# Attention plus MLP on one core: the final store as its own last piece, short dummy matmuls around the first transposes, the bias transpose later, and a new hand-written order

## The chip, the cores and the metric

The kernel runs on one core of a Trainium2 chip. The core has TensorE (PE, matrix multiplication; its weight loads are shown as PEld), VectorE (DVE), ScalarE (ACT), GpSimd (POOL) and SyncE (SP). Each works through its own queue in order and waits at semaphores for the others. DMAs are issued from the queues of SP, ACT and POOL. The metric is device microseconds of one execution. Before the change it is 217.93 us, the median of three runs (217.93 to 218.11).

## The reference, cut to what matters

One layer-normalised input feeds a windowed attention and an MLP; both results and the input are added. There are 2048 rows of 640 numbers, 32 heads of 20, and each row attends to 8 rows at distances 0, 2, ... 14 behind it.

```python
S, D, F, H, W, dil = 2048, 640, 1536, 32, 8, 2
xn = (x - mean(x)) / sqrt(var(x) + 1e-5)
q, k, v = split_heads(xn @ wqkv)                 # [H, S, 20] each
logits[h, s, w] = (q[h, s] . k[h, s - 2*w]) * 20**-0.5   # -1e9 where s < 2*w
attn = softmax(logits, axis=w)
o[h, s] = sum_w attn[h, s, w] * v[h, s - 2*w]
out = x + concat_heads(o) @ wo + (gelu(xn @ w1 + b1) @ w2 + b2)
```

All inputs and the output are bf16.

## The kernel before

The 2048 rows are cut into four chunks (0 to 3) of 512, and a chunk into four blocks of 128 rows. Everything on PE, DVE, ACT and SP is issued in an order that stands in the source as a list of piece names, `ORDER`; each name stands for one call of a small function, and each engine gets its instructions in the list's order. The framework adds the semaphores and the waiting for buffers. POOL's queue is not in that list's hands: its adding stores go out as their data become ready.

The names, with n the chunk and b the block in it:

- `st`, `su`, `sq`, `rs`, `rc`: statistics of the layer norm. For chunks 0 and 1 the sums are on DVE (`st`, `bn_stats`, L203), for block 1 of chunk 0 and chunks 2 and 3 on ACT. `rs` is the square root on ACT, `rc` the reciprocal on DVE.
- `xn`: the normalised block; on DVE for chunk 0 (L259), on ACT for the others (L257).
- `tp`, `tc`: for chunk 0 the transposes of xn on PE (L274) and their copies out of PSUM (L279; block 0's are in two parts, a and b, of which a is copied by DVE). In the other chunks `tc` is a transposing DMA issued on SP (L286).
- `ga`, `gb2` to `gb4`, `gd`, `ge`: q projections of blocks 0 and 1 of chunk 0, on PE, 50 matmuls of 128 columns (L331). `gc` copies them out on ACT.
- `hj` w p g and `hc` w p g: the other projections of chunk 0, by w (0 q, 1 k, 2 v), pair of blocks p and group of columns g, on PE with 256 columns (L362), and their copies on ACT (L372). Groups 0 and 1 have ten matmuls, group 2 has five.
- `pj` n w t and `pc` n w t: the projections of chunks 1 to 3, five matmuls of 512 columns each (L318), and their copies on ACT (L377).
- `qk` n b h: products of q with shifted k on DVE, half h of the window (L402). `pa` adds pairs of them (L420). `lg` sums them over the heads on PE into one PSUM tile of the tag L (L429), 24 matmuls, or 40 in chunk 1.
- `m`, `mx`, `ex`, `ss`, `ri`, `at`: the softmax, on DVE except `ex` on ACT. `xd` and `xs` spread attn over partitions by DMA, blocks 0 and 1 from SP, blocks 2 and 3 from ACT (L499).
- `av` n b h: attn times shifted v on DVE (L514); `ad` and `ot` add the products up (L523, L528) to oT.
- `f1` n_t and `ge` n_t: first layer of the MLP, five matmuls of 512 columns (L535), and GELU on ACT (L551).
- `o` n b c: output of a block, in five parts c: second layer of the MLP (0 to 3, three pairs of matmuls each) and the attention's projection (4, five pairs), with 512 columns into `lo` (L571) and 128 into `hi` (L573). For the last block of all the `hi` matmuls are one piece, `ohi`.
- `oc` n b and `od` n b: copy of a finished block to `osb` on ACT (L578, L579) and its adding store to DRAM on POOL (L584). There are two `osb` buffers.
- `oclo` and `ochi`: the last block is finished on DVE, where x is added (L592, L601), and stored plainly, the wide part from SP (L593), the narrow part from ACT (L604).
- `tb` and `b1`: the bias b1 is transposed on PE (L411) and copied by DVE to b1T (L414), which GELU reads.

ACT switches between tables for square root, exponential and GELU; each switch is a table load (L167) of 1.28 us. PSUM has four buffers of the tag acc (projections, first layer, transposes), one each for `lo` and `hi`, and one of the tag L, which the logits, `tb` and the dummy matmuls share.

Ahead of the list stand ten dummy matmuls of 512 columns on a constant of ones (L701), issued before any input has landed. The inputs are loaded from SP in this order: block 0 of x, wq, wk, blocks 2 and 3, wv, blocks 4 to 7, w1; block 1 and b1 from ACT.

## Time and profile before

| | |
|---|---|
| median of three runs | 217.93 us |
| profiled execution, whole | 219.77 us |
| its span, first to last instruction | 217.4 us |
| mean granted clock of PE | 0.994 |
| PE busy | 206.9 us (95%) |
| DVE busy | 179.2 us (82%) |
| ACT busy | 125.4 us (58%) |
| first matmul on a weight (L331) starts | 6.72 us |
| first qk on DVE (L402) starts | 19.34 us |
| ot3, the last large DVE piece, ends | 198.5 us |
| last matmul starts its group | 210.14 us |
| last store issued | 212.46 us |

Times inside the span count from its first instruction. A profile's row of the timeline gives start, length, engine, line, operation, what is written and read, shape, and in brackets how long the engine had been idle and what ended that. Matmuls are pipelined, so the time that one takes on PE is the distance to the start of the next, and the length shown is longer; holes are found from starts. The profiled execution is longer than the timed ones, so differences are worked out in the span and then set against the median.

### The profile page before, as it was taken

Reading aid. Unit: us, or ns where it says so; the run is one execution under the profiler, and the core shown is the slowest. Engines: PE = TensorE matmul, PEld = TensorE weight load, DVE = VectorE, ACT = ScalarE, POOL = GpSimd, SP = SyncE. Lnnn points to the kernel's source line nnn. Section 1 sums busy time; section 2 is a strip of 40 time slices with the busy share of each in tenths; the row PEclk is TensorE's granted clock in tenths of the full one; section 3 lists DMA queues with packets and bytes.
Section 4 is the critical chain, followed back from the end, with each engine's and each line's share of the span. In section 5 each row is a group of like instructions: output and inputs, shape, how many; then the busy total and the mean of one; then the engine's idle time right before and its main releaser. Section 6 shows DMA issues by size and latency. Waiting matters only on the chain.

```text
span 217.4 us, 3276 instructions
## 1 busy us (share of the span) xinstructions
PE 206.9 (95%) x1327; PEld 115.0 (53%) x1327; DVE 179.2 (82%) x166; ACT 125.4 (58%) x239; POOL 19.7 (9%) x37
## 2 busy tenths in 40 slices
PE   8999989999999998999999999999999999999970
PEld 2899635444645554555555544454555455555540
DVE  3578896599799999998999979996999999994010
ACT  5468595999989747689854558631844520111210
POOL 2000000000000500111010400000110101111301
PEclk9999999999999999999999999999999999999997
DMA  6991249418275996015521491702039202222232
GB/s 217 390 398 56 59 108 386 175 18 233 44 142 166 205 186 182 4 29 90 92 30 71 150 175 29 191 5 30 0 39 207 28 13 33 30 30 33 31 59 31
DMA packets 24069, 23.89 MB, mean 110 GB/s; under 512 B 9080, under 2 KB 21880, under 8 KB 24056
## 3 DMA queue, kind: packets, MB, share of 16 engines
q1 hardware_dynamic: 17008, 14.68, 23.3%
q0 software_dynamic: 4144, 4.92, 17.0%
q10 hardware_dynamic: 2904, 4.10, 5.9%
q8 instruction: 10, 0.16, 0.3%
q14 instruction: 3, 0.02, 0.0%
HBM read 10.00 MB, written 7.54 MB: 81 GB/s over the span
## 4 chain that ended last, share of the span: by engine, by line
PE 64%; DVE 13%; issue 11%; ACT 3%; DMA 3%; POOL 2%; ACTq 1%; POOLq 0%; SPq 0%
PE hps L535 19%; PE lo L571 17%; PE pps L318 15%; DVE half L514 5%; PE hi L573 4%; PE gps L362 3%; PE L L429 3%; DVE half L402 3%; DMA wq_sb<-in_A_wqkv_dram 3%; POOL out_dram L584 2%; PE gps L331 2%; DVE half L523 1%; DVE L L451 1%; DVE m L445 1%; ACTq L499 1%
## 5 line engine op out<-in xcount | busy, mean ns | idle before, releaser
L535 PE MATMUL hps<-xnT,w_sb 128*128 128x512 bf16 x240 | 55.4, 379 | 1.3 <-ACT hT L551 0.9
L402 DVE TENSOR_TENSOR half<-qT,kT 128x2560 bf16<-128x2560 bf16 x32 | 45.8, 1484 | 0.7 <-ACT kT L372 0.7
L571 PE MATMUL lo<-w_sb,hT 128*128 128x512 bf16 x144 | 41.0, 379 | 0.0
L535 PEld LDWEIGHTS <-w_sb 128*128 128x128 bf16 x240 | 22.9, 98 | 28.6 <-issue 2.5
L578 ACT CAST osb<-lo 128x512 bf16<-128x512 f32 x15 | 8.8, 585 | 42.7 <-issue 24.6
L573 PE MATMUL hi<-w_sb,hT 128*128 128x128 bf16 x144 | 31.5, 219 | 0.0
L551 ACT ACTIVATE hT<-hps,b1T 128x512 bf16<-128x512 f32 x36 | 23.5, 685 | 11.5 <-PE hps L535 11.5
L514 DVE TENSOR_TENSOR half<-vT,ax 128x2560 bf16<-128x2560 bf16 x16 | 23.1, 1478 | 1.2 <-PE L L429 1.2
L571 PEld LDWEIGHTS <-hT 128*128 128x128 bf16 x144 | 14.1, 98 | 17.2 <-issue 0.4
L571 PE MATMUL lo<-wo,oT 128*128 128x512 bf16 x80 | 23.1, 379 | 0.0
L584 POOL DMA_DIRECT2D out_dram<-osb x15 | 13.0, 864 | 110.0 <-ACT osb L579 94.1
L514 DVE TENSOR_TENSOR half<-vT,x_sb 128x2560 bf16<-128x2560 bf16 x16 | 22.6, 1483 | 0.0
L523 DVE TENSOR_TENSOR half<-half,half 128x5120 bf16<-128x5120 bf16 x8 | 22.3, 2813 | 0.1
L318 PE MATMUL pps<-xnT,wq_sb 128*128 128x512 bf16 x75 | 18.3, 379 | 1.0 <-ACT kT L377 1.0
L318 PE MATMUL pps<-xnT,wk_sb 128*128 128x512 bf16 x75 | 18.5, 379 | 0.0
L318 PE MATMUL pps<-xnT,wv_sb 128*128 128x512 bf16 x75 | 18.0, 379 | 0.0
L167 ACT ACT_TABLE_LOAD x13 | 16.7, 1283 | 1.0 <-PEq L719 0.7
L573 PE MATMUL hi<-wo,oT 128*128 128x128 bf16 x80 | 16.9, 219 | 0.0
L573 PEld LDWEIGHTS <-hT 128*128 128x128 bf16 x144 | 14.1, 98 | 1.7
L420 DVE TENSOR_TENSOR half<-half 128x2048 bf16<-128x2048 bf16 x12 | 14.1, 1216 | 0.0
L318 PEld LDWEIGHTS <-wq_sb 128*128 128x128 bf16 x75 | 8.7, 117 | 8.7 <-issue 1.6
L377 ACT CAST kT<-pps 128x512 bf16<-128x512 f32 x15 | 8.4, 590 | 7.7 <-PE pps L318 4.8
(86 smaller groups left out, 265.4 us busy)
## 6 DMA issues: line engine op xcount, KB each, us to landing
w_sb<-in_B_w_dram SPq DMA_DIRECT2D x4, 960.0 KB, 11.3
out_dram<-osb POOLq DMA_DIRECT2D x15, 160.0 KB, 3.4
out_dram<-b2bc POOLq DMA_DIRECT2D x3, 640.0 KB, 7.1
x_sb<-in_A_x_dram SPq DMA_DIRECT2D x1, 1280.0 KB, 7.8
out_dram<-x_sb ACTq DMA_DIRECT2D x1, 1120.0 KB, 4.8
ax<-attn SPq DMA_DIRECT2D x4, 256.0 KB, 4.3
ax<-attn ACTq DMA_DIRECT2D x4, 256.0 KB, 5.2
x_sb<-attn SPq DMA_DIRECT2D x4, 256.0 KB, 4.5
```

Source lines behind the costliest of these rows:

```text
L167: nc.scalar.activation(warm[:], nc.const_aps.tensor(0.0, [P, 1], F32), func)
L318: nc.tensor.matmul(ps[:], lhsT=wqkv_p[which][:, ti, to, :], rhs=xnT[:, ti, :], start=(ti == 0), stop=(ti == KT - 1),)
L402: nc.vector.tensor_tensor(out=half[h][:, :, :, cs], in0=qkv_tile(n, 0)[:, :, cs].unsqueeze(1).to_broadcast([P, W // 2, KT, P]), in1=window ...
L420: nc.vector.tensor_tensor(out=even, in0=even, in1=odd, op=ALU.add)
L514: nc.vector.tensor_tensor(out=half[h][:, :, :, cs], in0=window(qkv_tile(n, 2), h, cs), in1=ax_view(n)[:, j, ws, :].unsqueeze(2).to_broadca ...
L523: nc.vector.tensor_tensor(out=a, in0=a, in1=b, op=ALU.add)
L535: nc.tensor.matmul(ps[:], lhsT=w1_sb[:, ti, ft * P : (ft + 1) * P], rhs=tiles["xnT", n][:, ti, :], start=(ti == 0), stop=(ti == KT - 1),)
L551: nc.scalar.activation(hT, tiles["hps", n, ft][:], ACT.Gelu_apprx_tanh, bias=b1T[:, ft : ft + 1], scale=1.0)
L571: nc.tensor.matmul(lo[:], lhsT=lhs, rhs=rhs[:, 0:CH], start=first, stop=last)
L573: nc.tensor.matmul(hi[:, 0 : D - CH], lhsT=lhs, rhs=rhs[:, CH:D], start=first, stop=last)
L578: nc.scalar.copy(osb[:, 0:CH], tiles["lo", n, bl][:])
L584: nc.gpsimd.dma_start(rows, tiles["osb", n, bl][:], accum_op=ALU.add)
```

## The change

Five edits, and a new list.

1. The narrow store of the last block leaves `ochi` and becomes a piece of its own, `ochd`, which stands behind `ochi` and behind `oc30` in the new list.
2. The dummy matmuls become a function, `do_warm(n, cols)`. The ten of 512 columns stay, and three of 128 columns follow them ahead of the list.
3. Two new pieces issue more of them: `wa`, one of 128 columns between the transposes `tp00a` and `tp00b`, and `wb`, two of 128 columns behind `tp00b`.
4. `tb` and `b1` move from the middle of the first transposes to behind `ge`.
5. The rest of the list is in another order. The first pieces, to `ge`, keep theirs; behind them nearly all is moved.

```diff
@@ ORDER, its first lines
-pad01 pad02 st00a st00 sum1 rs00 mean1 neg1 rc00 sq1 xn00a xn00b tp00a tp00b tc00a rs01 tb ga tc00b rc01 xn01 gb2 b1
-tp01 gb3 tc01a tc01b gb4 gd gc0 ge st03a st03 rs03 gc1 hj100 st02a rc03 ho hc100 hj101 st02 rs02 hj201 xn03 tp03 rc02
-xn02 st11a st12a st11 st10a gc4 st13a tp02 hc101 tc03 tc02 hc201 hj102 hj200 hc200 hj011 hc102 st10 hc011 st13 st12
-rs1 rc1 qk000 qk001 xn12 tc12 hj112 hc112 xn11 qk011 hj010 hc010 tc11 hj111 hj110 hj202 hc202 hc111 qk010 pa010 hj012
-hc012 hc110 qk021 qk030 qk031 xn10 qk020 pa011 hj211 hc211 tc10 hj212 f10_11 f10_2 xn13 tc13 hc212 ge0_2 f10_9 ge0_9
-f10_0 ge0_0 f10_6 pj114 ldx ld2 pj100 ge0_6 pc100 pj110 pc110 pj102 pad11 pa000 pj112 pa001 lg0 mask m0 ge0_11 pc114
+pad01 pad02 st00a st00 sum1 rs00 mean1 neg1 rc00 sq1 xn00a xn00b tp00a wa tp00b wb tc00a rs01 ga tc00b rc01 xn01 gb2
+tp01 gb3 tc01a tc01b gb4 gd gc0 ge tb b1 st02a hj100 st03a hc100 st02 hj101 rs02 hj200 st03 rs03 gc1 hc101 hc200 rc02
+xn02 ho tp02 gc4 hj202 rc03 tc02 xn03 tp03 st12a st10a st11a tc03 st10 st13a st11 hc202 hj201 hc201 hj102 hc102 hj112
+hj012 hc112 st12 st13 rs1 rc1 qk001 hj212 hc212 xn12 tc12 qk000 qk011 xn11 tc11 hj110 hj111 hc110 hj011 qk010 hc111
+hc012 hc011 hj010 hc010 qk021 f10_3 f10_6 xn10 tc10 xn13 qk020 qk030 f10_0 ge0_0 f10_9 ge0_9 qk031 f10_2 ge0_2 f10_11
+ge0_11 tc13 ldx pj102 ge0_6 pj104 ge0_3 pc102 pj112 pj103 pad11 pa000 pc104 pa011 pa001 pj101 pa010 lg0 pc112 mask m0
...
@@ ORDER, around the second softmax
-f10_8 av030 ge0_8 xn20 f11_5 ge1_5 o001 o002 o003 tc21 ex1 pj122 av021 xp0 xb0 ss1 pj120 xp1 pc122 tc20 pj211 pc211
-xb1 av031 pc120 su32 ri1 ad00 pj204 pc204 at1 xd1 ad01 ad02 ot0 pj203 pad12 av111 pc203 av101 su30 pj222 pc222 pj224
-pc224 pj221 pc221 xs1 av121 pj212 pc212 pj220 pc220 pj223 pj202 pc202 pc223 pj213 pc213 pad22 su33 pj201 f11_1 pc201
+ge0_10 ge0_7 f11_8 ge1_8 tc22 o001 tc20 ex1 f11_5 ss1 av010 ri1 pj120 pc120 ge1_5 o002 o003 av011 at1 xp1 xb1 pj211
+pc211 pj202 ad00 pc202 f11_10 ad01 ad02 pj212 pad12 pj214 su31 pc214 ge1_10 ot0 pad21 pj201 xd1 pc201 pj210 pj223
+pc223 pj222 pc210 pc222 pj221 pc221 av101 xs1 pj213 av121 pc212 pc213 pad31 pj220 pj200 pc220 su32 su30 su33 ng3 av100
...
@@ ORDER, its end
-o323 ot3 o324 oc32 od32 o314 o300 o334 o301 o302 o303 o304 ohi oc31 od31 oclo ochi oc30 od30
+ad31 ad32 ot3 o324 oc32 o314 od22 od32 oc31 od31 o300 o301 o302 o303 o304 oc30 o332 o333 o334 oclo ohi ochi ochd od30
@@ new function
+    ones = nc.const_aps.tensor(1.0, [P, CH], BF16)
+    idle = psL.tile([P, W, P], F32, tag="L", name="idle")
+
+    def do_warm(n, cols):
+        for _ in range(n):
+            nc.tensor.matmul(
+                idle[:].rearrange("p w c -> p (w c)")[:, 0:cols],
+                lhsT=ones[:, 0:P],
+                rhs=ones[:, 0:cols],
+                start=True,
+                stop=True,
+            )
@@ do_ochi and do_ochd
-        nc.scalar.dma_start(out_sd[LASTB * P :, CH:D], osb[:, CH:D])
+
+    def do_ochd():
+        nc.scalar.dma_start(out_sd[LASTB * P :, CH:D], tiles["osb", last][:, CH:D])
@@ pieces
+    piece("wa", do_warm, 1, P)
+    piece("wb", do_warm, 2, P)
@@ ahead of the list
-        ones = nc.const_aps.tensor(1.0, [P, CH], BF16)
-        idle = psL.tile([P, W, P], F32, tag="L", name="idle")
-        for _ in range(WARM):
-            nc.tensor.matmul(idle[:, 0:BPC, :], lhsT=ones[:, 0:P], rhs=ones, start=True, stop=True)
+        do_warm(WARM, CH)
+        do_warm(3, P)
```

More of the change, by code (lines that the diff above doesn't have):

```diff
@@ L44 @@
-f10_0 ge0_0 f10_6 pj114 ldx ld2 pj100 ge0_6 pc100 pj110 pc110 pj102 pad11 pa000 pj112 pa001 lg0 mask m0 ge0_11 pc114
-mx0 pc112 pj111 pc102 su22 su20 ex0 ss0 pj103 pj113 pc103 pc111 pc113 pj104 pc104 pj101 pc101 ri0 at0 f10_1 qk110
-qk130 f11_9 qk120 su23 f10_10 qk101 ge1_9 su21 f11_10 ge0_10 ge0_1 ng2 f11_3 ge1_3 sq21 f10_4 ge0_4 sq23 f11_0 ge1_0
-pj124 pc124 qk121 sq22 f11_7 ge1_7 f10_7 xd0 qk100 qk131 sq20 pj121 ge0_7 rs2 hj210 hc210 qk111 xs0 lg1 ldo rc2 pc121
-xn23 av001 tc23 m1 pj123 pc123 av000 xn22 av010 f10_5 av020 av011 mx1 f11_4 o000 ge0_5 ge1_10 xn21 f10_3 ge0_3 tc22
@@ L49 @@
-f10_8 av030 ge0_8 xn20 f11_5 ge1_5 o001 o002 o003 tc21 ex1 pj122 av021 xp0 xb0 ss1 pj120 xp1 pc122 tc20 pj211 pc211
-xb1 av031 pc120 su32 ri1 ad00 pj204 pc204 at1 xd1 ad01 ad02 ot0 pj203 pad12 av111 pc203 av101 su30 pj222 pc222 pj224
-pc224 pj221 pc221 xs1 av121 pj212 pc212 pj220 pc220 pj223 pj202 pc202 pc223 pj213 pc213 pad22 su33 pj201 f11_1 pc201
-su31 av110 pj210 o004 oc00 od00 pj214 av100 pad21 pc214 pc210 ng3 sq31 av130 o020 o021 av131 av120 o022 o023 sq30 sq32
-o024 oc02 sq33 rs3 rc3 pj200 pc200 xn31 tc31 o030 o031 o032 o033 o034 xn30 tc30 oc03 ad10 od03 f11_6 o010 o011 o012
@@ L54 @@
-ge1_4 xn32 pad31 ad11 tc32 ad12 o013 qk211 xn33 f12_0 o014 f12_4 ge1_1 ge1_6 oc01 od01 ot1 qk221 ge2_0 qk230 qk231
-qk220 qk210 ge2_4 qk201 pa211 pa210 f11_2 ge1_2 tc33 pj320 pj304 pc304 qk200 pa201 pj301 pc301 pj324 pj310 pc324 pa200
-pj303 pc303 pj323 pc323 pad32 pc320 pj312 pj302 xp2 pc302 pj314 pc314 pc312 xl pj313 pj300 pc313 pj311 f13_6 lg2 pc311
-m2 pc310 ge3_6 o130 pc300 qk310 mx2 f11_8 ge1_8 f12_10 o131 o132 qk321 ex2 ss2 ri2 at2 qk301 qk330 qk320 qk331 qk300
-f13_11 pa311 f13_5 ge3_5 f13_10 ge3_10 ge2_10 qk311 ge3_11 f13_4 f13_0 xs2 f13_3 ge3_3 pa300 ge3_4 ge3_0 f11_11 ge1_11
@@ L59 @@
-f12_8 f12_9 pa301 ge2_8 f13_8 ge3_8 pj322 o133 o134 oc13 od13 pc322 f13_1 ge3_1 pa310 o110 o111 o112 lg3 m3 xd2 av210
-xb2 mx3 f12_3 ge2_3 av211 ex3 ss3 f12_7 f13_2 o113 o114 oc11 od11 od02 f13_7 ge3_7 av200 ri3 o100 av230 o101 o102 o103
-xb3 ge3_2 o104 oc10 at3 xs3 f12_6 av231 o120 f12_2 ge2_2 av201 av221 ge2_9 ge2_7 o121 o122 av220 o123 od10 f12_5 ge2_5
-f12_11 o124 oc12 od12 ad20 ad21 ad22 ot2 pj321 pc321 av331 xd3 av300 av301 av321 f12_1 ge2_1 av311 ge2_6 f13_9 o210
-ge3_9 o211 ge2_11 o212 o213 o310 o214 oc21 od21 o330 o331 o200 o201 o202 o203 o204 oc20 od20 o311 o312 o220 o221 o222
@@ L64 @@
-av330 av310 o223 o224 o313 av320 ad30 oc22 od22 ad31 ad32 o230 o231 o232 o233 o234 oc23 od23 o332 o333 o320 o321 o322
-o323 ot3 o324 oc32 od32 o314 o300 o334 o301 o302 o303 o304 ohi oc31 od31 oclo ochi oc30 od30
+pad01 pad02 st00a st00 sum1 rs00 mean1 neg1 rc00 sq1 xn00a xn00b tp00a wa tp00b wb tc00a rs01 ga tc00b rc01 xn01 gb2
+tp01 gb3 tc01a tc01b gb4 gd gc0 ge tb b1 st02a hj100 st03a hc100 st02 hj101 rs02 hj200 st03 rs03 gc1 hc101 hc200 rc02
+xn02 ho tp02 gc4 hj202 rc03 tc02 xn03 tp03 st12a st10a st11a tc03 st10 st13a st11 hc202 hj201 hc201 hj102 hc102 hj112
@@ new lines @@
+hj012 hc112 st12 st13 rs1 rc1 qk001 hj212 hc212 xn12 tc12 qk000 qk011 xn11 tc11 hj110 hj111 hc110 hj011 qk010 hc111
+hc012 hc011 hj010 hc010 qk021 f10_3 f10_6 xn10 tc10 xn13 qk020 qk030 f10_0 ge0_0 f10_9 ge0_9 qk031 f10_2 ge0_2 f10_11
+ge0_11 tc13 ldx pj102 ge0_6 pj104 ge0_3 pc102 pj112 pj103 pad11 pa000 pc104 pa011 pa001 pj101 pa010 lg0 pc112 mask m0
+pc103 pc101 mx0 ld2 pj100 su20 su21 pc100 ex0 ss0 pj111 pj113 pc113 pj114 pc114 pc111 ri0 pj110 pc110 qk101 su23 at0
+qk131 xd0 f11_0 ge1_0 su22 f10_1 f10_5 ge0_5 qk100 qk111 pj122 pc122 ng2 xs0 pj121 f10_8 ge0_8 sq20 f11_3 ge1_3 sq21
@@ new lines @@
+hj211 hc211 qk121 hj210 hc210 pj123 sq22 ge0_1 qk130 qk120 qk110 sq23 ldo pj124 rs2 o000 rc2 pc121 lg1 av031 av021
+av000 xp0 m1 xb0 av001 mx1 f10_4 av020 av030 f10_7 xn21 tc21 pc123 xn23 pc124 ge0_4 xn22 f11_9 tc23 ge1_9 xn20 f10_10
+ge0_10 ge0_7 f11_8 ge1_8 tc22 o001 tc20 ex1 f11_5 ss1 av010 ri1 pj120 pc120 ge1_5 o002 o003 av011 at1 xp1 xb1 pj211
+pc211 pj202 ad00 pc202 f11_10 ad01 ad02 pj212 pad12 pj214 su31 pc214 ge1_10 ot0 pad21 pj201 xd1 pc201 pj210 pj223
+pc223 pj222 pc210 pc222 pj221 pc221 av101 xs1 pj213 av121 pc212 pc213 pad31 pj220 pj200 pc220 su32 su30 su33 ng3 av100
@@ new lines @@
+f11_2 pj204 pc204 av111 av120 pj203 o004 av131 oc00 od00 pad22 pj224 sq33 pc224 sq30 av130 o020 o021 o022 o023 sq32
+o024 f11_11 oc02 o030 o031 o032 o033 sq31 rs3 pc200 av110 od02 rc3 xn32 xn33 tc32 ad11 f11_6 pc203 o034 oc03 od03
+f12_1 o010 o011 o012 o013 ge1_11 f11_4 tc33 xn30 xn31 tc30 tc31 ge2_1 ge1_6 ad10 ad12 o014 qk211 ge1_4 f12_5 ge2_5 ot1
+qk201 qk230 f11_7 pj303 ge1_2 pc303 qk220 pj313 ge1_7 qk200 qk221 pc313 pa210 pj302 pc302 pj300 pc300 qk231 qk210
+pa211 pa200 pj310 pj311 pc311 pj314 oc01 pad32 od01 pc310 pc314 f13_6 pj324 pj320 pc320 pj312 pa201 f11_1 ge3_6 pj304
@@ new lines @@
+ge1_1 xl lg2 pc324 m2 mx2 pc304 pj301 pc301 pc312 qk331 qk320 o130 o131 ex2 ss2 qk321 ri2 at2 xd2 qk311 qk330 o132
+f12_10 f12_6 ge2_6 qk300 f13_11 pa311 qk301 ge3_11 f13_7 ge3_7 f12_4 qk310 pa301 o133 pa310 o134 xp2 ge2_4 oc13 od13
+f13_3 xs2 ge3_3 f13_10 ge3_10 f12_0 f13_1 ge3_1 xb2 f13_5 o120 pj323 o121 o122 o123 o124 oc12 pa300 lg3 pc323 ge3_5 m3
+av201 mx3 av220 ge2_0 ex3 ss3 o110 av210 ri3 av211 f12_7 o111 f13_9 ge3_9 o112 o113 o114 oc11 xb3 f13_0 ge3_0 f13_2
+od11 ge3_2 ge2_7 pj322 pc322 o100 o101 f12_2 ge2_2 od12 f12_11 ge2_11 at3 xd3 av230 f13_8 ge3_8 av221 f12_3 ge2_10
@@ L66 @@
+ge2_3 o102 o103 xs3 av200 f13_4 pj321 pc321 o104 oc10 av231 ad21 ad20 f12_8 ad22 ot2 o210 ge2_8 f12_9 av311 o310 o211
+o212 od10 ge2_9 ge3_4 o213 o214 oc21 od21 av330 o311 o200 av320 o201 o202 o203 av331 av321 av300 o204 oc20 od20 o312
+av301 o230 o231 o232 o233 av310 o234 o313 oc23 od23 o220 o221 o222 o223 o224 oc22 o330 o331 o320 o321 ad30 o322 o323
+ad31 ad32 ot3 o324 oc32 o314 od22 od32 oc31 od31 o300 o301 o302 o303 o304 oc30 o332 o333 o334 oclo ohi ochi ochd od30
 """.split()
@@ L610, in piece @@
         pieces[name] = lambda: fn(*args)
-    for name in "tb b1 mean1 ho ldx ld2 ldo xl oclo ohi ochi mask".split():
+    for name in "tb b1 mean1 ho ldx ld2 ldo xl oclo ohi ochi ochd mask".split():
         piece(name, locals()[f"do_{name}"])
```

## The prediction

> **What bounds the kernel now.** I read the page first (shares, chain), then the tail, the head and the holes of TensorE in order of time.

> ```profile
> PE 206.9 (95%) x1327; PEld 115.0 (53%) x1327; DVE 179.2 (82%) x166; ACT 125.4 (58%) x239; POOL 19.7 (9%) x37
> PE 64%; DVE 13%; issue 11%; ACT 3%; DMA 3%; POOL 2%; ACTq 1%; POOLq 0%; SPq 0%
> out_dram<-osb POOLq DMA_DIRECT2D x15, 160.0 KB, 3.4
> out_dram<-osb SPq DMA_DIRECT2D x1, 128.0 KB, 1.7
> out_dram<-osb ACTq DMA_DIRECT2D x1, 32.0 KB, 1.5
> ```

> TensorE (PE) carries the chain. A 512-column matmul starts every 0.216 us, so its work is fixed; what an order can change is the time before the first one, the holes, and the time after the last. The three store rows price the end: an adding store from POOL lands 3.4 us after issue, a plain one after 1.5 to 1.7. The timeline of the tail (start, length, engine):

> ```profile
> 210.14 0.44 PE L573 MATMUL hi<-wo,oT 128*128 128x128 bf16 x5
> 210.62 0.29 DVE L601 TENSOR_TENSOR osb<-hi,x_sb 128x128 bf16<-128x128 f32 x1 [2.81 <-PE hi L573]
> 210.94 0.35 ACTq L604 DMA_DIRECT2D out_dram<-osb  x1
> 211.41 0.58 ACT L578 CAST osb<-lo 128x512 bf16<-128x512 f32 x1 [6.70 <-DVE osb L601]
> 212.46 0.86 POOL L584 DMA_DIRECT2D out_dram<-osb  x1 [6.59 <-ACT osb L579]
> ```

> PE ends at 210.6 (call it E). The copy oc30 had its sums from o304 by then, but stands behind the store of L604 on ACT and starts at 211.41; its adding store goes out at 212.46 and lands near 215.9. The span ends at 217.4, 1.5 later, which is the closing work. So E to landing is 5.3.

> Head, and the holes of PE:

> ```profile
> 9.00:10.00 1.00, 1.00 (x12) 1.00 (x10) 0.70 (x2) 0.48 (x1) 0.00 (x0) 1.00 1.06 396
> 10.00:11.00 1.00, 1.00 (x21) 1.00 (x19) 0.96 (x4) 0.83 (x2) 0.00 (x0) 1.00 1.07 397
> 9.59 0.89 DVE L203 BATCH_NORM_STATS2 stats<-x_sb 128x6 f32<-128x320 bf16 x2 [0.21 <-DMA x_sb<-in_A_x_dram]
> 11.35 2.35 PE L362 MATMUL gps<-xnT,wk_sb 128*128 128x256 bf16 x20
> 19.34 4.29 DVE L402 TENSOR_TENSOR half<-qT,kT 128x2560 bf16<-128x2560 bf16 x3
> 23.66 0.58 ACT L372 CAST kT<-gps 128x512 bf16<-128x512 f32 x1 [0.69 <-DVE half L402]
> 24.84 1.24 PE L535 MATMUL hps<-xnT,w_sb 128*128 128x512 bf16 x5
> 26.44 3.61 PE L535 MATMUL hps<-xnT,w_sb 128*128 128x512 bf16 x15 [0.36 <-ACT kT L372]
> 30.91 1.24 PE L535 MATMUL hps<-xnT,w_sb 128*128 128x512 bf16 x5 [0.85 <-ACT hT L551]
> 79.50 2.32 PE L318 MATMUL pps<-xnT,wv_sb 128*128 128x512 bf16 x10
> 82.79 1.24 PE L318 MATMUL pps<-xnT,wq_sb 128*128 128x512 bf16 x5 [0.96 <-ACT kT L377]
> ```

> The first two rows are stretches of one microsecond (PE busy and count lead): 12 matmuls of 128 columns to 10.0, 21 after it. Their spacing falls from 107 to 56 ns at 10.0, so PE ran at half speed until then, though the clock column shows 1.00. Holes by spacing: 24.84 + 5 x 0.216 = 25.92, next start 26.44: 0.52. 26.44 + 15 x 0.216 = 29.68, next 30.91: 1.23. 79.50 + 10 x 0.216 = 81.66, next 82.79: 1.13. With 0.2 near 24.7 and 0.2 near 43 that is all of size; elsewhere PE has no hole to win.

> **The change, part by part.** Sums are made on the profiled execution: span 217.4 in 219.77, so 2.35 around it. The timed median, 217.93, is 1.84 below that; I take differences from the span and put them on the median.

> *Last store.* New end: o304, oc30, o332 to o334, ohi, then ochd, last on ACT. oc30 now runs under the 11 lo matmuls and 17 hi matmuls that follow o304: 11 x 0.216 + 17 x 0.056 = 3.33. Its store goes out 1.05 after o304 (211.41 to 212.46 now), at E - 2.3, and lands at E + 1.1. The lo part: o334 ends at E - 0.95, 0.69 on DVE (L592), 1.7 to land: E + 1.5. The hi part: 0.32 to its issue (210.62 to 210.94), 1.5 to land: E + 1.8, the last. So 5.3 becomes 1.8: -3.5; I take **-3.4**. Were the last store to need 3.4 like the adding ones, it would be -1.6. Behind ochd on ACT and SP stands only the closing. The two osb buffers don't bind: oclo needs od31's, which is issued near E - 6.9 and lands at E - 3.5, and oclo starts at E - 0.9.

> *Short matmuls.* Three at the start, at 0.107 (0.32 in all), fill the 0.26 that PE waited for xn at 5.46; the one and the two around the transposes lie before wq, which lands near 6.7 (PE idled 0.35 for it). On the path: 0 to 0.1; if wq came earlier, 0.3. Their gain is unknown. From 6.72 to 10.0 PE issued 31 matmuls at 107 ns; at 56 they would take 1.58 less. So the price lies between 0 and -1.58 (a later opening is excluded: PE does no less before 10.0). I take 0: dense matmuls from 0.78 to 5.05, 4.3 us, did not open the clock before, and this adds 0.64 to them, with transposes in between; what opened it was 3.3 us of dense real work.

> [...]

> *Bias transpose behind the first projections.* This is the costly one. tb on PE now follows ge, and b1 on VectorE (DVE) stands ahead of st02a, st03a and every other statistic. DVE took the rows of x at 9.59 when they landed. Now it waits for ge (11.35), tb 0.19, b1 0.16: it starts near 11.75. From 9.59 to the first qk it needed 9.75, with waits of 1.07 (rstd of block 2) and 0.92 in it; the first goes and about half of the second, since the order of the statistics is better. First qk: 11.75 + 9.75 - 1.07 - 0.45 = 20.0 against 19.34, 0.65 late. PE loses 0.1 for tb.

> *New order at 22 to 32.* Three qk end 4.29 after the first, at 24.3, and hc110, which overwrites kT, waits for them as the copy at 23.66 did; it ends near 24.9. PE from 11.45 has 95 matmuls of 256 columns at 0.109 and ten transposes at 0.056, 10.9 in all, and some 0.2 of waits: done near 22.6. The four PSUM banks then hold hj012 (its copy now stands behind hc110 and hc111 on ACT), hj110, hj111, hj011, so hj010 waits for hc110: 2.3. Next hj010 1.09, to 26.0; f10_3 needs hc111, which waits for qk010 (24.95 to 26.43) and ends at 27.0: 1.05. The GELU table load (1.28, as at 30.91 now) stalls one more first-layer group: about 0.6, less than now since three groups stand ahead. Sum 3.95 against 0.2 + 0.52 + 1.23 = 1.95: **+2.0**. Bounds: 0.65 (the lateness of qk alone) to 3.

> *New order later.* The hole at 82.79 came from ACT waiting for attn before xs1 and issuing it for 2.3. Now eight projection copies and a GELU stand between at1 and xs1 on ACT, 9 us of PE work, so attn is there first: -1.1. The 0.2 at 43 goes. Against them the late DVE makes lg1 wait: in the new order qk1 is one piece longer in coming, while PE has used its cover; I put 0.7 (0 to 1.5; lg0 left DVE idle for 3.1 before, so DVE has room). One table load more, 14 for 13, at 1.28 on ACT (58% busy) is free behind four banks. Together **-0.6**.

> Sum: -3.4 + 0.1 + 2.0 - 0.6 = -1.9. E goes from 210.6 to 212.1, the end from 217.4 to 215.5.

> **Forecast A**, 52%: 217.93 - 1.9 = **216.0**, own range 215.2 to 217.0.

> **Rivals.** *B, the clock opens one step earlier* (30%). For it: PE has no hole over 0.1 from 0.78 to 6.3. Against: the 4.3 us that did not open it. Everything on PE and DVE up to the first qk shifts: 216.0 - 1.58 = 214.4.

> *C, DVE becomes the bound* (10%), the slower side. Place: qk021 waits for hc111, hc012, hc011, hc010 in a row on ACT (to 28.4, where DVE is free at 26.4). Before, it started at 26.83 with pa010 (1.13) done, which now comes later, so DVE is 1.6 + 1.1 = 2.7 behind there. Behind ot3, which ends at 198.5 now (197.00 and 1.49), PE has 10.7 of work in the new order (o324 1.36, o314 1.36, o300 to o304 4.62, 3.33), so E = 198.5 + late + 10.7. At 2.9 late this equals A's E; each further microsecond counts in full, and over 5.4 late the kernel is slower. Another 3 would have to come from attn, sent from ACT by a later place in the list (landing 5.2 to 5.7). At 6: E 215.2, end 218.5, time 219.0. Against it: in the view of waits DVE idled 3.1 for lg0 and 3.5 for two of the other logits, which takes up lateness.

> *D, the last store does not pay* (4%): if another store, or the closing, ends last, the -3.4 is gone and the head's cost stays: 217.93 + 1.5 = 219.4. The remaining 4% is a mix near 217.9.

> **Numbers.** This kernel's measurement tells 0.2% (0.44 us) from no change. Faster: A, B and part of the rest, 0.85; same 0.03; slower (C, D) 0.12. The range from 214.2 to 217.2 takes in B whole and A's unknown sizes, and leaves out C and D.

> **What would show it.** After: last PE end to span end near 3.3 (right) or over 5 (D). Spacing of the L331 matmuls falling to 56 ns at 10.0 (A) or by 6.8 (B). DVE idle some 2 us ahead of b1; first qk near 20.0 (A) or 18.4 (B). A PE hole over 2 us ahead of the last q projection near 25, none near 82. ot3 ending within 1.5 us of o324 means that C is close. I am wrong if the hole near 25 is under 1 us, or PE's last end is outside 210 to 213.

## The result and the profile after

| | before | changed |
|---|---|---|
| median | 217.98 us (12 runs) | 216.89 us (12 runs, 216.25 to 220.13) |
| ratio, 95% interval | 1 | 0.9944 (0.9922 to 0.9966) |
| profiled execution, whole | 219.77 us | 218.16 us |
| its span | 217.4 us | 215.9 us |
| mean granted clock of PE in it | 0.994 | 0.992 |

The kernel is faster by 0.56%, 1.2 us by the ratio (0.7 to 1.7). The ratio leaves out two slow runs of the changed kernel, 219.78 and 220.13 us, which its median holds. The forecast was 1.9. From here on a ratio is turned into microseconds with 217.98 us. The changed kernel's profiled execution is 1.27 us longer than its median, and it shows more holes than the others.

The page of the changed kernel: shares, the clock in 40 slices, the chain of work that ended last.

```profile
PE 205.8 (95%) x1311; PEld 115.3 (53%) x1333; DVE 179.0 (83%) x166; ACT 126.8 (59%) x241; POOL 19.8 (9%) x37
PEclk9999699999999999999999999999999999999999
PE 81%; DVE 6%; ACT 6%; DMA 2%; ACTq 2%; issue 1%
```

PE still sets the end. New is the 6 in the fifth slice of the clock (21.6 to 27.0 us). Some twenty matmul records are missing in this trace, so a start distance of exactly two matmuls is not read as a hole.

The timeline of its tail (start, length, engine, line, operation, in brackets the idle time before):

```profile
209.84 0.59 ACT L592 CAST osb<-lo 128x512 bf16<-128x512 f32 x1 [3.87 <-PE hi L587]
210.88 0.86 POOL L598 DMA_DIRECT2D out_dram<-osb  x1 [3.76 <-ACT osb L593]
212.69 0.44 PE L587 MATMUL hi<-wo,oT 128*128 128x128 bf16 x5
213.00 0.35 SPq L607 DMA_DIRECT2D out_dram<-osb  x1
213.17 0.29 DVE L615 TENSOR_TENSOR osb<-hi,x_sb 128x128 bf16<-128x128 f32 x1 [0.20 <-PE hi L587]
213.49 0.36 ACTq L620 DMA_DIRECT2D out_dram<-osb  x1
```

oc30 (209.84) now runs while PE still works, and its adding store leaves 2.25 us before PE's end (213.13). The last store is the plain one of 213.49. From PE's end to the span's end it is 2.8, where it was 6.8.

The head, first in stretches of one microsecond (PE busy and its matmuls lead), then as a timeline, from 5 to 34 us:

```profile
6.00:7.00 1.00, 1.00 (x18) 1.00 (x16) 0.73 (x3) 0.61 (x2) 0.00 (x0) 1.00 1.06 396
7.00:8.00 1.00, 1.00 (x22) 1.00 (x20) 0.29 (x1) 0.07 (x1) 0.00 (x0) 1.00 1.06 392
```

```profile
9.57 2.38 PE L362 MATMUL gps<-xnT,wk_sb 128*128 128x256 bf16 x20
9.68 0.17 DVE L428 CAST b1T<-tb 128x12 f32<-128x12 bf16 x1 [1.77 <-PE tb L425]
17.80 4.29 DVE L402 TENSOR_TENSOR half<-qT,kT 128x2560 bf16<-128x2560 bf16 x3
19.49 1.26 PE L362 MATMUL gps<-xnT,wq_sb 128*128 128x256 bf16 x10
22.18 0.58 ACT L372 CAST kT<-gps 128x512 bf16<-128x512 f32 x1 [2.53 <-DVE half L402]
22.82 1.75 PE L362 MATMUL gps<-xnT,wq_sb 128*128 128x256 bf16 x10 [2.07 <-ACT kT L372]
24.38 0.58 ACT L372 CAST kT<-gps 128x512 bf16<-128x512 f32 x1 [1.61 <-DVE half L402]
25.82 4.55 PE L549 MATMUL hps<-xnT,w_sb 128*128 128x512 bf16 x18 [0.22 <-issue]
```

22 matmuls of 128 columns in a microsecond already from 7.0: the clock opened at 6.4, not at 10.0, and the first 256-column projection starts at 9.57 (11.35 before). Then comes the hole that was forecast: the last matmul before it starts at 20.48, ACT holds hc110 back until the third qk has read kT (2.53 of waiting), and hj010 starts at 22.82: 2.24 us of empty PE. What was not forecast stands in the matmuls after it. The first six of hj010 are 0.109 us apart, as 256 columns were before; from 23.5 on they are 0.213 apart. The windows of that place, 3.41 us each:

```profile
20.01:23.42 3.41, 1.34 (x13) 1.18 (x12) 2.70 (x3) 0.58 (x1) 0.00 (x0) 1.00 0.43 96
23.42:26.84 3.42, 2.75 (x10) 1.38 (x10) 1.46 (x2) 2.46 (x5) 0.00 (x0) 0.50 0.01 2
```

The first figure behind the length is PE's busy time, the third from the right the granted clock: 1.00, then 0.50. After a stretch in which PE was busy for only 1.34 of 3.41 us the clock stood at half for exactly one stretch.

Later on:

```profile
79.80 2.97 PE L318 MATMUL pps<-xnT,wv_sb 128*128 128x512 bf16 x12
82.60 1.24 PE L318 MATMUL pps<-xnT,wk_sb 128*128 128x512 bf16 x5
139.36 3.22 ACTq L513 DMA_DIRECT2D ax<-attn  x1
140.24 2.93 POOL L299 DMA_DIRECT2D out_dram<-b2bc  x2
143.37 1.89 PE L549 MATMUL hps<-xnT,w_sb 128*128 128x512 bf16 x8 [1.47 <-ACT wq_sb L565]
```

The hole near 82 is gone, as forecast. In its place this execution has one of 1.5 us at 141.8: ACT was 3.22 us in issuing one transfer of attn while POOL issued two of its own, and its GELU came late. The kernel without the short matmuls (a4 below, the same order) has 0.07 there, and b3 0.19, so most of it is this execution's and not the order's.

### The profile page after: what moved, and what is told of

It reads as the page before. It is cut to its first block, busy times and chain, and to the rows that moved or that the text cites. A ratio compares the mean times of both kernels' runs of the same rounds, so it can differ in the third digit from the quotient of the medians.

```text
span 215.9 us, 3264 instructions
## 1 busy us (share of the span) xinstructions
PE 205.8 (95%) x1311; PEld 115.3 (53%) x1333; DVE 179.0 (83%) x166; ACT 126.8 (59%) x241; POOL 19.8 (9%) x37
## 4 chain that ended last, share of the span: by engine, by line
PE 81%; DVE 6%; ACT 6%; DMA 2%; ACTq 2%; issue 1%
PE lo L585 25%; PE pps L318 22%; PE hps L549 19%; PE hi L587 8%; DVE half L402 3%; PE idle L415 2%; DMA xnT<-xn 2%; DVE stats L203 2%; PE L L443 2%; ACTq L513 2%; PE gps L331 1%; ACT xn L257 1%; ACT hT L565 1%; ACT trash L222 1%; ACT L167 1%
## 5 line engine op out<-in xcount | busy, mean ns | idle before, releaser
L549 PE MATMUL hps<-xnT,w_sb 128*128 128x512 bf16 x236 | 56.1, 382 | 2.4 <-ACT wq_sb L565 1.5
L402 DVE TENSOR_TENSOR half<-qT,kT 128x2560 bf16<-128x2560 bf16 x32 | 45.8, 1483 | 2.7 <-ACT qT L372 2.0
L585 PE MATMUL lo<-w_sb,hT 128*128 128x512 bf16 x136 | 39.6, 379 | 0.0
L592 ACT CAST osb<-lo 128x512 bf16<-128x512 f32 x15 | 8.8, 585 | 39.2 <-issue 22.6
L528 DVE TENSOR_TENSOR half<-vT,x_sb 128x2560 bf16<-128x2560 bf16 x16 | 22.6, 1484 | 0.0
L318 PE MATMUL pps<-xnT,wv_sb 128*128 128x512 bf16 x73 | 17.7, 379 | 0.9 <-ACT hT L565 0.7
L318 PE MATMUL pps<-xnT,wq_sb 128*128 128x512 bf16 x73 | 17.9, 380 | 0.1
L318 PE MATMUL pps<-xnT,wk_sb 128*128 128x512 bf16 x73 | 17.5, 379 | 0.1
L318 PEld LDWEIGHTS <-wv_sb 128*128 128x128 bf16 x75 | 8.7, 117 | 8.2 <-issue 1.2
L318 PEld LDWEIGHTS <-wq_sb 128*128 128x128 bf16 x75 | 8.7, 118 | 7.9 <-issue 0.8
## 6 DMA issues: line engine op xcount, KB each, us to landing
w_sb<-in_B_w_dram SPq DMA_DIRECT2D x4, 960.0 KB, 11.4
```

The costliest lines, as they stand in the source:

```text
L318: nc.tensor.matmul(ps[:], lhsT=wqkv_p[which][:, ti, to, :], rhs=xnT[:, ti, :], start=(ti == 0), stop=(ti == KT - 1),)
L402: nc.vector.tensor_tensor(out=half[h][:, :, :, cs], in0=qkv_tile(n, 0)[:, :, cs].unsqueeze(1).to_broadcast([P, W // 2, KT, P]), in1=window ...
L528: nc.vector.tensor_tensor(out=half[h][:, :, :, cs], in0=window(qkv_tile(n, 2), h, cs), in1=ax_view(n)[:, j, ws, :].unsqueeze(2).to_broadca ...
L549: nc.tensor.matmul(ps[:], lhsT=w1_sb[:, ti, ft * P : (ft + 1) * P], rhs=tiles["xnT", n][:, ti, :], start=(ti == 0), stop=(ti == KT - 1),)
L585: nc.tensor.matmul(lo[:], lhsT=lhs, rhs=rhs[:, 0:CH], start=first, stop=last)
L592: nc.scalar.copy(osb[:, 0:CH], tiles["lo", n, bl][:])
```

## The experiments

Twelve kernels, each timed against before in five rounds.

**One part alone, one part undone.** a1 is before with the new end only:

```diff
-av330 av310 o223 o224 o313 av320 ad30 oc22 od22 ad31 ad32 o230 o231 o232 o233 o234 oc23 od23 o332 o333 o320 o321 o322
-o323 ot3 o324 oc32 od32 o314 o300 o334 o301 o302 o303 o304 ohi oc31 od31 oclo ochi oc30 od30
+av330 av310 o223 o224 o313 av320 ad30 oc22 od22 ad31 ad32 o230 o231 o232 o233 o234 oc23 od23 o320 o321 o322 o323 ot3
+o324 oc32 od32 o314 oc31 od31 o300 o301 o302 o303 o304 oc30 o332 o333 o334 oclo ohi ochi ochd od30
...
-        nc.scalar.dma_start(out_sd[LASTB * P :, CH:D], osb[:, CH:D])
+
+    def do_ochd():
+        nc.scalar.dma_start(out_sd[LASTB * P :, CH:D], tiles["osb", last][:, CH:D])
```

> The kernel before with the new end alone: ochd behind oc30, and o332, o333, o334 behind o304. If the tail pays as reckoned, the 6.8 us from PE's last end to the span's end shrink to about 3 (the changed kernel showed 2.8), against a loss of up to 0.8 because o332 and o333 no longer cover PE's wait for ot3: 2.6 to 4.0 us faster than before, 214.0 to 215.4 us. If another store ends last (rival D): 218 us, unchanged.

Measured: 215.01 us, 0.9839 (0.9792 to 0.9886), 3.5 us less than before (2.5 to 4.5), and less than the changed kernel too. PE ends at 209.90 in a span of 212.7: 2.8 behind PE again.

a2 is before with the six short matmuls only:

```diff
-tp00a tp00b tc00a
+tp00a wa tp00b wb tc00a
...
+        do_warm(3, P)
```

> The kernel before with the six short dummy matmuls alone. Forecast A (they do not open the clock): 218.0 us, L331 spacing falls to 56 ns near 10.0 us. Rival B (they do, as the changed kernel's profile shows, with 56 ns from 6.4 us): the first L362 starts near 9.7 instead of 11.35 and the time falls by 1.6 to 216.4 us. A third way: the timed executions of the kernel before open early anyway, and only its profiled one was late; then the profile shows 6.4 and the time stays at 218.0.

Measured: 218.34 us, 0.9987 (0.9956 to 1.0018): nothing. The clock opened at 5.1 in it, but at 5.3 in a1 too, which has none of the short matmuls.

a3 is the changed kernel with oc30 back behind the store on ACT:

```diff
-o304 oc30 o332 o333 o334 oclo ohi ochi ochd od30
+o304 o332 o333 o334 oclo ohi ochi ochd oc30 od30
```

> The changed kernel with oc30 put back behind ochd on ACT. If the tail is what pays: 3.4 to 4.1 us slower than the changed kernel (216.9), so 220.3 to 221.0 us, and slower than before. If the new order pays and the tail does not: 216.9.

Measured: 222.23 us, 1.0133 (1.0076 to 1.019). Against the changed kernel the old end costs 1.89%, 4.1 us, give or take 1.3.

a4 is the changed kernel without the six short matmuls:

```diff
-tp00a wa tp00b wb tc00a
+tp00a tp00b tc00a
...
-        do_warm(3, P)
```

> The changed kernel without the six short dummy matmuls. If they open the clock: the first L362 starts near 11.4 instead of 9.6 and the time is 1.6 us more, 218.5 us. If they do nothing: 216.9 us.

Measured: 217.80 us, 0.9948 (0.9914 to 0.9982); with them it is 0.9944. They do nothing here either. So the end is worth 3.5 to 4.1, the short matmuls nothing, and the new order with the moved bias transpose costs over 2 us (a4 against a1: 2.4, give or take 1.3).

**Which half of the order.** Both lists have nearly the same pieces up to qk021, so they can be spliced there. c1 takes before's list up to qk021 and the new one behind it, c2 the reverse; both have the new end and no short matmuls, like a1 (old, old) and a4 (new, new).

```diff
@@ c1 against a4, all up to qk021
-tp01 gb3 tc01a tc01b gb4 gd gc0 ge tb b1 st02a hj100 st03a hc100 st02 hj101 rs02 hj200 st03 rs03 gc1 hc101 hc200 rc02
...
-hc012 hc011 hj010 hc010 qk021 f10_3 f10_6
+tp01 gb3 tc01a tc01b gb4 gd gc0 ge st03a st03 rs03 gc1 hj100 st02a rc03 ho hc100 hj101 st02 rs02 hj201 xn03 tp03 rc02
...
+hc012 hc110 qk021 hj212 hc212 f10_3 f10_6
```

> The end of the change and its order after the last qk of the first block (qk021), with the order of before up to there (bias transpose early, no short matmuls). Theory H (the first 33 us of the new order cost what the end brings: the 2.2 us hole of PE, the half-speed stretch behind it, the late vector work): near the order of before with the new end, 0.982 to 0.988 of before, with no half-speed stretch between 20 and 30 us. Theory L (the later order costs it: the profile of the changed kernel has 4.2 us of holes there, 2.4 more than before): 0.993 to 0.997, like the changed kernel.

Measured: 215.26 us, 0.9848 (0.9824 to 0.9873). The clock was at 1.0 in all five executions.

> The reverse: the new order up to qk021, the order of before behind it, the new end, no short matmuls. Theory H: 0.993 to 0.998 of before, a hole over 2 us between 20 and 24 us and the clock closed for one stretch behind it. Theory L: 0.982 to 0.988, holes in the later part under 2 us in sum. If both cost half, both splices stand near 0.989.

Measured: 216.89 us, 0.9938 (0.9904 to 0.9972), with a hole of 2.24 at 20.4 and a half-speed stretch from 23.06 to 26.47. The four corners:

| order up to qk021 | order behind it: before's | new |
|---|---|---|
| before's | a1 0.9839 | c1 0.9848 |
| new | c2 0.9938 | a4 0.9948 |

The new head costs 0.0099 and 0.0100, 2.2 us, whatever follows it. The new later order costs 0.0009 and 0.0010, which the intervals don't tell from nothing. c1, c2 and the two below ran beside one set of runs of before, a1 to a4 beside another.

**What in the head.** b1_bias_early puts tb and b1 of the changed kernel back to where they stood:

```diff
-rs01 ga
+rs01 tb ga
...
-gb2 tp01
+gb2 b1 tp01
...
-ge tb b1 st02a
+ge st02a
```

> The changed kernel with the bias transpose and its sum back at their places of before (tb ahead of ga, b1 ahead of tp01). Theory T (the wait of VectorE for tb, 1.77 us in the profile, makes the first qk late and so the hole of PE near 21 us): first qk 1.3 to 1.8 earlier than the 17.8 of the changed kernel, hole at most 1 us, time 0.985 to 0.989 of before. Rival (the place of hc110 ahead of the q copies makes the hole, whatever the bias does): hole still 1.5 to 2.3, time within 0.4 us of the changed kernel, 0.993 to 0.996.

Measured: 217.18 us, 0.9934 (0.991 to 0.9958): no difference. Its timeline on DVE and ACT:

```profile
9.72 1.28 DVE L203 BATCH_NORM_STATS2 stats<-x_sb 128x6 f32<-128x320 bf16 x3 [1.23 <-DMA x_sb<-in_A_x_dram]
22.64 0.58 ACT L372 CAST kT<-gps 128x512 bf16<-128x512 f32 x1 [2.53 <-DVE half L402]
```

DVE no longer waits for tb, but then for the rows of x, until the same 9.7. The wait of 2.53 ahead of hc110 is unchanged. In these two profiles, where the clock opened early, the moved bias transpose cost nothing, because ge was done by the time the rows landed (9.46 against 9.7).

b2 moves the q copies ahead of hc110:

```diff
-hj110 hj111 hc110 hj011 qk010 hc111 hc012 hc011 hj010 hc010 qk021
+hj110 hj111 hj011 hc012 hc011 hj010 hc010 hc110 qk010 hc111 qk021
```

> The changed kernel with the q copies hc012, hc011, hc010 and the projection hj010 ahead of the k copy hc110 (on ScalarE the copies that need nothing go first). Rival of the bias theory (place of hc110): no hole over 0.5 us at 20 to 23 us, no half-speed stretch there, 1.0 to 2.5 us less than the changed kernel (0.983 to 0.990 of before), unless the gap comes back ahead of the first GELU. Theory T: the hole stays over 1 us, 0.993 to 0.996.

Measured: 215.94 us, 0.9886 (0.9842 to 0.993), 1.3 us less than the changed kernel (0.2 to 2.3). Timeline of PE and ACT:

```profile
22.28 4.71 PE L549 MATMUL hps<-xnT,w_sb 128*128 128x512 bf16 x20
22.96 0.59 ACT L372 CAST kT<-gps 128x512 bf16<-128x512 f32 x1
25.11 0.58 ACT L372 CAST kT<-gps 128x512 bf16<-128x512 f32 x1 [1.56 <-DVE half L402]
27.34 1.28 ACT L167 ACT_TABLE_LOAD   x1
29.46 1.89 PE L549 MATMUL hps<-xnT,w_sb 128*128 128x512 bf16 x8 [2.48 <-ACT hT L565]
```

The hole at 20.5 is gone, so the place of hc110 on ACT made it. PE has now done its four first-layer groups earlier and waits 2.5 for the first GELU, whose table load comes late.

b3 leaves the changed kernel's order and fills the hole with nine 512-column matmuls on ones, ahead of hj010:

```diff
-hj011 qk010
+hj011 wf qk010
...
+    def do_fill(n):
+        fill[0] = psL.tile([P, W, P], F32, tag="L", name="fill")
+        for _ in range(n):
...
+    piece("wf", do_fill, 9)
```

> The changed kernel with nine 512-column matmuls on ones (1.94 us at 0.216) put into the hole of PE ahead of hj010, in an accumulator that nothing else uses; nothing that is computed changes. Theory G (the empty PE, by closing the clock for one 3.41 us stretch, costs 0.7 on average and up to 1.7): the clock column has no closed stretch near 20 to 30 us, the mean clock of nearly all executions 0.999 or 1.0, time 0.6 to 1.2 us less than the changed kernel, 0.989 to 0.992 of before. Rival (the hole itself is the whole cost, the half-speed stretch falls where PE would wait anyway): same as the changed kernel, 0.993 to 0.996, even with the clock open.

Measured: 216.11 us, 0.9901 (0.9881 to 0.9921), 0.9 us less than the changed kernel (0.3 to 1.6), from work that nobody uses. Its PE:

```profile
21.03 1.91 PE L655 MATMUL fill<-const-bfloat16-1.0 128*128 128x512 bf16 x8
23.05 1.25 PE L362 MATMUL gps<-xnT,wq_sb 128*128 128x256 bf16 x10
25.25 4.48 PE L549 MATMUL hps<-xnT,w_sb 128*128 128x512 bf16 x20 [0.95 <-ACT kT L372]
30.22 2.32 PE L549 MATMUL hps<-xnT,w_sb 128*128 128x512 bf16 x10 [0.49 <-ACT hT L565]
```

The useful hj010 starts no earlier than in the changed kernel, but all ten of its matmuls are spaced 0.109. The clock was 0.999 or 1.0 in all six executions. In the four kernels with the new head and an empty hole (the changed one, a4, b1_bias_early, c2) it was 0.998 or more in only 14 of 48, and 0.992 (one closed stretch: 3.41 x 0.5 / 216 = 0.008) or less in the others.

**Versions that might be better.** e1 is b2 with the GELU table loaded by a warming activation ahead of hc110:

```diff
-hc010 hc110
+hc010 tg hc110
...
+    def do_tg():
+        table(ACT.Gelu_apprx_tanh)
```

> The q copies first as in the run before, and the load of the GELU table (1.28 us, with its 0.20 warming activation) put ahead of the k copy hc110, where ScalarE waits 1.56 for the qk products. If the 2.6 us hole ahead of the fourth first-layer group near 27 us comes from the late GELU: it shrinks to 1.0 to 1.4, and the time is 1.0 to 1.5 us below the q-first run, 0.981 to 0.985 of before, so the head of the new order is then as good as that of before. If the hole is DVE's (qk021 late): unchanged, 0.987 to 0.990.

Measured: 215.80 us, 0.9888 (0.9867 to 0.9909). Missed, and the mistake was in the expectation: ACT's wait of 1.56 in b2 stands ahead of the copy at 25.11, which is hc111. hc110, at 22.96, waited for nothing, so the load went in front of work that was due. e1's timeline:

```profile
22.46 1.28 ACT L167 ACT_TABLE_LOAD   x1
23.87 0.57 ACT L372 CAST kT<-gps 128x512 bf16<-128x512 f32 x1
24.47 1.49 DVE L402 TENSOR_TENSOR half<-qT,kT 128x2560 bf16<-128x2560 bf16 x1 [2.39 <-ACT kT L372]
```

hc110 is 0.91 later (23.87 for 22.96), and DVE with it; PE's one gap of 2.5 became three of 0.5 to 1.0.

d1 is a1 with the same load ahead of hc110, where in a1 ACT does wait (1.28, to 24.22):

```diff
-hc012 hc110 qk021
+hc012 tg hc110 qk021
```

> The order of before with the new end alone, and the load of the GELU table put ahead of hc110, where ScalarE waits 1.28 us for the qk products there. Hole of PE at 28 us (1.01) shrinks to 0 to 0.3, hc110 0.2 later: 0.6 to 0.9 us less than the run with the new end alone (0.9839), 0.980 to 0.982 of before. Rival (VectorE sets the pace behind it): no gain, 0.983 to 0.986.

Measured: 214.28 us, 0.9825 (0.9802 to 0.9847). The hole of 1.01 at 28.3 is gone; but 0.0014 of the ratio, 0.3 us, is less than expected, and lies within the interval of a1, so a gain in time isn't shown.

d2 is d1 with all four transfers of attn issued by SP:

```diff
-        expand(nc.scalar, n, (2, 3))
+        expand(nc.sync, n, (2, 3))
```

> As the run before, and all four transfers that spread attn over the partitions are issued by SP instead of two by ACT. If the 1.2 us hole of PE at 79.9 comes from ACT holding its copies while it issues xs1: gone, 0.8 to 1.2 us less than the run before, 0.975 to 0.978 of before. Rival (SP's four in a row land later and make VectorE's products late): hole gone, but the same time or up to 1 us more.

Measured: 212.51 us (212.36 to 213.11), 0.9746 (0.9724 to 0.9769): the best of all, 5.5 us below before and 1.7 below d1 (1.0 to 2.4), for a hole of 1.2. What it removes, in a1's timeline and then in d2's:

```profile
78.20 2.41 ACTq L499 DMA_DIRECT2D x_sb<-attn  x2
80.65 0.59 ACT L377 CAST kT<-pps 128x512 bf16<-128x512 f32 x1 [3.03 <-issue]
81.29 1.24 PE L318 MATMUL pps<-xnT,wq_sb 128*128 128x512 bf16 x5 [1.05 <-ACT kT L377]
```

```profile
77.33 4.11 SPq L499 DMA_DIRECT2D x_sb<-attn  x4
79.20 1.24 PE L318 MATMUL pps<-xnT,wq_sb 128*128 128x512 bf16 x5
80.28 1.24 PE L318 MATMUL pps<-xnT,wk_sb 128*128 128x512 bf16 x5
```

SP issues for 4.11 us and nothing behind it is missed; ACT's copies run on, and PE has no hole. In both kernels the same four transfers are issued at the same place; only the engine that has copies queued behind them differs.

## Why the prediction came out as it did

The forecast was 216.0 in a range of 214.2 to 217.2, against 216.89; it took 1.9 off where 1.2 came off. Step by step:

- **Last store, -3.4.** Right. Measured alone -3.5, undone from the changed kernel -4.1. In the profile PE's end to the span's end fell to 2.8, where 3.3 was expected.
- **Short matmuls, 0.** Right: a2 and a4 show none. Rival B was right about what the clock does (it opened at 6.4, L331's spacing was 56 ns by 7) and wrong about the gain. The clock opened between 3.6 and 6.4 us in all thirteen profiles of the changed kernel and its relatives, with and without the short matmuls, in a1 with the very head of before. So the late opening in the first profile of before, at 9.99, was most likely a trait of that one execution, 1.84 us above its own median. I had put the differences on the median and escaped the error; B, which took 1.58 off it, counted a loss that, by a2's time, most of the timed runs can't have had.
- **Bias transpose: PE +0.1, first qk 0.65 later.** DVE waited 1.77 for tb, as forecast, but b1_bias_early shows that it would have waited for x's rows until 9.7 anyway. The first qk starts at 17.80 in the changed kernel and at 17.75 in a1. The step rested on ge ending at 11.35, a figure of the late clock.
- **New order at 22 to 32, +2.0.** This is the step that failed, in what it left out. Its holes were forecast well. With the clock held open (b3) they are all there: 2.24 before hj010 (forecast 2.3), 1.1 before f10_3 (1.05), 0.65 before a later first-layer group (0.6), and b3 stands at 0.9901, 2.2 below before; the forecast sum was 1.9. What was put at nothing is the clock: it was closed for at least one stretch in 34 of 48 executions with that hole (mean of 0.992 or less), and that costs 0.9 us by the pair of b3 and the changed kernel. That +2.0 nevertheless stands close to the +2.2 of the corners is luck. With the clock open the new head costs only 1.2 (b3 against c1, which have the same later order; 0.5 to 1.9): the order of before loses more here than the 1.95 that I took from its first profile, 2.4 in a1 and 2.9 in c1, where the clock opened early. The closed clock then adds about what was priced too dear.
- **New order later, -0.6.** The hole near 82 did go. By time the later half costs 0.2 (c1 against a1, a4 against c2), give or take 1.1 in each pair, so not even its sign is known. In the profiles of a1 and c1 the holes behind 34 us shrink from 2.3 to 1.6, but the one near 27 us, where the later list begins, grows from 1.0 to 1.8. That this is where the 0.6 went is read from single executions, not shown by an experiment.

The parts measured are -3.5 for the end, +2.2 for the head, +0.2 for the rest: -1.1, against a measured -1.2. They are steps between the corners and so lead to a4 by themselves; that a4 and the changed kernel agree is the measurement. Split this way the head's two errors cancel, and what the forecast lacks stands in the later order, within its intervals. What doesn't depend on the split is the whole: 2.2 off with the clock open (b3), 1.2 off in the changed kernel.

Rival C (DVE becomes the bound) and rival D (the last store doesn't pay) did not come about. I had named two signs of being wrong. The hole was 2.2, not under 1; but PE's last end, 213.13, lies 0.13 outside the bounds that I gave. That execution has both the closed clock and the hole at 141.8, and either is larger than 0.13; in b3, which has the clock open and 0.19 there, PE ends at 211.1.

## What to carry over

Measure the parts of a change alone before taking it whole: the new end is worth 1.6% by itself, and the reordering that came with it gave two thirds of that back. In an in-order queue, look at what a copy that must wait (here hc110, for the readers of its buffer) holds up behind it, and at whether a DMA issue of a microsecond stands ahead of copies on which PE waits; with the new end, these issues moved to an idle queue brought 1.7 us and the best time, 212.51; a table load put into a wait that is really there took away a hole, but no time that the intervals show. Price a hole of PE not at its own length only: where it left PE busy for 1.25 to 1.34 of the 3.41 us of a clock stretch, in five profiles here, the next stretch ran at half speed.

## What the hardware showed that I had not expected

```profile
25.69:29.10 3.41, 1.54 (x8) 0.62 (x7) 2.76 (x3) 3.11 (x5) 0.00 (x0) 1.00 0.18 42
29.10:32.51 3.41, 3.41 (x10) 1.22 (x9) 3.41 (x4) 0.95 (x2) 0.00 (x0) 0.50 0.56 111
```

In e1 1.54 of 3.41 closed it (second row: clock 0.50); in b2 it stayed open at 1.43, behind a hole of 2.5 us that fell across a border:

```profile
27.47:30.89 3.42, 1.43 (x7) 0.68 (x7) 3.42 (x3) 2.66 (x5) 0.00 (x0) 1.00 0.57 109
```

Behind stretches with 1.95 or more it stayed open in all fourteen profiles. The phase also bears on the opening. In the first profile of before a border fell at 6.58, and this stretch, with six transposes among its matmuls, did not open the clock:

```profile
3.17:6.58 3.41, 2.95 (x11) 0.92 (x9) 2.65 (x10) 2.72 (x8) 0.00 (x0) 1.00 1.03 365
```

In b2 a first stretch with 2.81 us of the dummy matmuls alone opened it. Whether the transposes or the waits between them made the difference was not tried.

The matmuls on ones in b3 kept the clock open: PE was busy for 3.30 of the 3.41 us from 19.59, the next stretch stood at 1.00, and the mean was 0.999 or 1.0 in all six executions.

A second thing: issuing one 256 KB transfer from ACT took 0.57 us at 138.76 and 3.22 at 139.36, when POOL issued two of its own beside it. POOL's issue alone is not the cause: in the other kernels with the new later order it stands there too, and ACT's transfer took 1.6 to 2.5; in a4 POOL began the same 0.88 us after ACT, and ACT took 1.66. What made it 3.22 in this one execution is open.
